# Sigmoid attention and a gated feed-forward: the first loads by SyncE in FP32, cast on ScalarE and VectorE, and the first pass in a new order

## The chip, the cores and the metric

The kernel runs on one core of one Trainium2 chip. The metric is the device time of one execution in microseconds. The time before is the median of three runs, 376.28 us (376.24 to 376.35). All positions below are microseconds from the start of the profiled span.

## What is computed

q, k and v have the shape (8, 12, 448, 64): 8 batches, 12 heads, 448 positions, 64 per head. All inputs and the output are FP32.

```python
scores = np.matmul(q, k.transpose(0, 1, 3, 2)) / np.sqrt(64) - np.log(448)
attn = 1 / (1 + np.exp(-scores))                 # a sigmoid, no softmax
x = np.matmul(attn, v)                           # heads put side by side: (3584, 768)
h = x @ w_in                                     # (3584, 2048)
out = (h / (1 + np.exp(-beta * h))) @ w_out      # (3584, 768)
```

## The kernel before, in words

**Tiles.** Heads are handled in 24 groups of four (three groups per batch). A group's q and k stand in one tile `raw` of 128 partitions, 32 for each head; each partition holds 14 blocks of 64 numbers. `load_one` (L122) loads q (in whole or one half of 7 blocks) or k of a group with a DMA that GpSimd issues and that turns FP32 into FP16 on the way. `transpose` (L201) makes `qT` and `kT` from it with VectorE's stream transposes (L207 for q; L216 and L220 for k, the first for 384 positions and the second for the last 64).

**A score visit.** `half_visit` (L294) does the scores of one group for one half of the queries (224 of 448). With `second` = 0 it does the first 256 keys, with `second` = 1 the other 192. It takes two pairs of PSUM banks, issues 16 matmuls of 32 rows (L236), and `weigh` (L247, ScalarE, L249) or `weigh_two` (L258, L264) writes the sigmoids to one or two of 14 slots of `attns`. At first three pairs of banks serve the scores (`share_psum(3)`), and from `("two",)` on two pairs.

**Values and the dense layers.** `attend` (L316) multiplies sigmoids with v (L334), and VectorE copies the result to `xT` (L343). `dense1` (L349) is the first dense layer in units of one matmul (L356); each sixth unit closes a block, whose sigmoid (ScalarE, L368) and product (VectorE, L371) go to the tile `gt`. `dense2` (L381, matmul L386) is the second layer. Later batches use products with fewer matmuls (L510, L628), which the change doesn't touch. All units of dense work stand in a list `fill`, in order; `fill_units(n)` issues the next n. The first batch has 48 units of 224 columns (blocks 0 to 7, first half of the queries), and then pairs of blocks at 448 columns, alternating with the other halves of earlier blocks.

**Order of the work.** Each engine runs its instructions in the order of the program, and this order is written out by hand. The first pass is the list `BEGIN` (L791): `("q", g, half)` and `("k", g)` are transposes, `("scores", g, half, second)` a score visit, `("values", g, half)` an `attend`, `("v", 0)` a copy inside v on VectorE (`double_v_last`, L168), `("beta",)` four small transposes, `("dense", n)` the next n units, and `("idle", n)` n matmuls on zeros (L751). Eleven more zero matmuls stand ahead of the list. Groups 0, 1 and 2 are one batch. After `BEGIN` a planner spreads the rest of `fill` over the visits of the later groups: it divides the work left by the number of visits left in a phase, with corrections by hand (`MORE`, `LATE`, L849 to L856).

**Loads.** GpSimd's queue carries, in this order: first half of q and all of k of group 0, two memsets, the list `LOADS` (L767), and at `("loads",)` those of `loads()` (L775). SyncE's queue carries one early load, `beta_in` (L766), and later all stores of the output. The tiles `raw` exist three times, so that group 3 takes the place of group 0.

Of the kernel before, what the change touches and what calls it, by code (L numbers as in the profile page):

```python
# [8 lines left out]
FP32 = mybir.dt.float32  # L9
FP16 = mybir.dt.float16  # L10
# [3 lines left out]
def kernel(  # L14
# [10 lines left out]
    nc = tc.nc  # L25
# [3 lines left out]
    B, H, S, D = q.shape  # L29
    NTOK, DM = out.shape  # L30
    DFF = moe_w_in.shape[1]
    P = 128
    BLK = 32
    HQ = P // BLK
    NB = S // BLK
# [19 lines left out]
    rawp = ctx.enter_context(tc.tile_pool(name="rawp", bufs=3))  # L55
# [29 lines left out]
    def bank(cols: int = S, hold=None, at=None):  # L85
        if at is None:
            at = min((i for i in used if i not in held.values()), key=used.get)
        assert at not in held.values()
        touch(at)
        if hold is not None:  # L90
            held[hold] = at
        width[at] = cols
        return ps[:, at, 0:cols]
# [25 lines left out]
    raws = {}  # L119
    vs = {}  # L120

    def load_one(g: int, r: int, c0: int = 0, c1: int = NB):  # L122
        b, t = divmod(g, QPB)
        if g not in raws:
            raws[g] = rawp.tile([P, 2, NB, D], FP16, tag="raw", name="raw")
        nc.gpsimd.dma_start(  # L126
            out=raws[g][:, r, c0:c1].rearrange("p c d -> p (c d)"),
            in_=(q, k)[r][b, HQ * t : HQ * (t + 1)].rearrange("h (p c) d -> (h p) (c d)", c=NB)[
                :, c0 * D : c1 * D
            ],  # L130
        )

    def load_qk(g: int):
        load_one(g, 0)
        load_one(g, 1)
# [7 lines left out]
    def load_v_full(b: int, lo: int = 0, hi: int = H):  # L143

        if b not in vs:
            vs[b] = vp.tile([P, H, JF + 1, D], FP16, tag="v16", name="v16")
        rows = v[b, lo:hi].rearrange("h (p c) d -> p h (c d)", c=NB)
        for i in range(HQ):
            nc.gpsimd.dma_start(
                out=vs[b][i * BLK : (i + 1) * BLK, lo:hi, 0:JF].rearrange("p h j d -> p h (j d)"),  # L150
                in_=rows[:, :, JF * i * D : JF * (i + 1) * D],
            )
            ready.update((b, "full", t, i) for t in range(lo // HQ, hi // HQ))

    def load_v_last(b: int):
        if b not in vs:
            vs[b] = vp.tile([P, H, JF + 1, D], FP16, tag="v16", name="v16")
        rows = v[b].rearrange("h (p c) d -> p h c d", c=NB)
        for c in range(NF, NB):
            lo = (c - NF) * BLK  # L160
            nc.gpsimd.dma_start(out=vs[b][lo : lo + BLK, :, JF], in_=rows[:, :, c])
        ready.add((b, "last"))

    def load_v(b: int):
        load_v_full(b)
        load_v_last(b)

    def double_v_last(b: int):  # L168
        assert (b, "last") in ready
        ready.add((b, "v"))  # L170
        nc.vector.tensor_copy(out=vs[b][KL:P, :, JF], in_=vs[b][0:KL, :, JF])
# [3 lines left out]
    def load_w_in(lo: int, hi: int):  # L175

        nc.gpsimd.dma_start(
            out=w_in16[:, :, lo * P : hi * P],
            in_=moe_w_in[:, lo * P : hi * P].rearrange("(c p) f -> p c f", p=P),
        )  # L180

    def load_w_out(c: int, half: int):
        n = NDC // WOUT
        cols = slice(half * HALF, (half + 1) * HALF)
        nc.gpsimd.dma_start(
            out=w_out16[:, c * n : (c + 1) * n, cols],
            in_=moe_w_out[c * n * P : (c + 1) * n * P, cols].rearrange("(c p) f -> p c f", p=P),
        )
# [5 lines left out]
    ready = set()  # L194


    def in_order(b: int, t):
        t = t.rearrange("p c e -> p (c e)").bitcast(FP32)
        return t.rearrange("p (q c) -> p c q", c=NB) if b == B - 1 else t

    def transpose(g: int, r: int, c0: int = 0, c1: int = NB):  # L201
        raw = raws[g][:, r]
        if r == 0:
            if g not in qT:
                qT[g] = qTp.tile([P, NB * BLK, PAIR], FP16, tag="qT", name="qT")
            ready.update((g, "q", c) for c in range(c0, c1, NB // 2))
            nc.vector.transpose(  # L207
                out=in_order(g // QPB, qT[g][:, c0 * BLK : c1 * BLK]),
                in_=raw[:, c0:c1].rearrange("p c d -> p (c d)").bitcast(FP32),
            )  # L210
            return
        ready.add((g, "k"))
        kT[g] = kTp.tile([P, S, PAIR], FP16, tag="kT", name="kT")
        to = kT[g].rearrange("p k e -> p (k e)").bitcast(FP32)
        frm = raw.rearrange("p c d -> p (c d)").bitcast(FP32).rearrange("p (c f) -> p c f", c=NB)
        nc.vector.transpose(  # L216
            out=to[:, 0 : JF * P].rearrange("p (j i q) -> p i j q", j=JF, i=HQ),
            in_=frm[:, 0:NF].rearrange("p (i j) f -> p i j f", j=JF),
        )
        nc.vector.transpose(  # L220
            out=to[:, JF * P :], in_=frm[:, NF:].rearrange("p c f -> p (c f)")
        )
# [123 lines left out]
    gt = const.tile([P, NDC, WIN], FP16, name="gt")  # L346
# [388 lines left out]
    NH = NB // 2  # L735
    share_psum(3)
    with tc.manual_schedule():
        load_one(0, 0, 0, NH)
        load_one(0, 1)
        nc.gpsimd.memset(nlogs, NEG_LOG_S)  # L740
        nc.gpsimd.memset(dummy, 0.0)
        nc.scalar.activation(out=dummy, in_=dummy, func=AF.Sigmoid, bias=0.0, scale=1.0)
# [4 lines left out]
        idle = bank(512)  # L747

        def idle_units(n: int):
            for _ in range(n):  # L750
                nc.tensor.matmul(idle, still[:, 0:P], still, start=True, stop=True)  # L751

        idle_units(11)
        def load(what, *a):
            if what == "q":
                load_one(a[0], 0, a[1] * NH, (a[1] + 1) * NH)
            elif what == "k":
                load_one(a[0], 1)
            elif what == "v":
                load_v_full(0, a[0] * HQ, a[1] * HQ)  # L760
            elif what == "last":
                load_v_last(0)
            elif what == "w_in":
                load_w_in(*a)

        nc.sync.dma_start(out=beta_in[0:NDC], in_=moe_beta.rearrange("(c p) -> c p", p=P))  # L766
        LOADS = [  # L767
            ("q", 1, 0), ("k", 1), ("q", 2, 0), ("k", 2), ("last",), ("v", 0, 3), ("q", 0, 1), ("q", 1, 1),
            ("w_in", 0, 2), ("w_in", 2, 4), ("q", 2, 1), ("w_in", 4, 6), ("w_in", 6, 8), ("w_in", 8, 10),
            ("w_in", 10, 12), ("w_in", 12, 14), ("w_in", 14, 16),  # L770
        ]
        for x in LOADS:
            load(*x)

        def loads():  # L775
            load_qk(3)
            load_w_out(0, 0)
            load_w_out(1, 0)
            load_v(1)
            load_qk(4)  # L780
            load_qk(5)
            load_w_out(0, 1)
            load_w_out(1, 1)

        def beta_columns():
            ready.add("beta")
# [2 lines left out]
                nc.vector.transpose(out=beta_sb[part], in_=beta_in[:, part])  # L789

        BEGIN = [  # L791
            ("q", 0, 0), ("k", 0), ("q", 1, 0), ("scores", 0, 0, 1), ("idle", 4), ("k", 1), ("idle", 4),
            ("scores", 0, 0, 0), ("k", 2), ("q", 2, 0), ("scores", 1, 0, 0), ("idle", 4), ("v", 0),
            ("scores", 1, 0, 1), ("scores", 2, 0, 0), ("values", 0, 0), ("q", 0, 1), ("q", 1, 1),
            ("scores", 2, 0, 1), ("beta",), ("values", 1, 0), ("scores", 0, 1, 0), ("values", 2, 0),
            ("scores", 0, 1, 1), ("loads",), ("q", 2, 1), ("dense", 12), ("scores", 1, 1, 1), ("two",),
            ("dense", 6), ("scores", 1, 1, 0), ("dense", 18), ("scores", 2, 1, 0), ("values", 0, 1),
            ("values", 1, 1), ("scores", 2, 1, 1), ("dense", 9), ("values", 2, 1), ("dense", 42), ("k", 3),
            ("q", 3, 0), ("q", 3, 1), ("dense", 21),
        ]  # L800
        for what, *a in BEGIN:
            if what == "q":
                g, half = a
                transpose(g, 0, half * NH, (half + 1) * NH)
            elif what == "k":
                transpose(a[0], 1)
            elif what == "scores":
                half_visit(a[0], a[1] * QH, a[2])
            elif what == "idle":
                idle_units(a[0])  # L810
            elif what == "v":
                double_v_last(a[0])
            elif what == "values":
                attend(a[0], a[1] * QH, QH, a[2:] or (0, 1))
            elif what == "dense":
                fill_units(a[0])
            elif what == "beta":
                beta_columns()
            elif what == "loads":
                loads()  # L820
            elif what == "two":
                share_psum(2)
# [153 lines left out]
```

## Time and profile before

| | before |
|---|---|
| median of three runs | 376.28 us |
| the profiled execution | 375.9 us |
| its span, first to last instruction | 374.1 us |
| TensorE busy | 366.0 us, 98% |
| ScalarE busy | 254.8 us, 68% |
| VectorE busy | 254.3 us, 68% |
| GpSimd busy | 91.4 us, 24% |
| first k of group 0: issue, landing | 1.95, 5.51 |
| first score matmul | 6.17 |
| first score sigmoid on ScalarE | 6.92 |
| start of the matmul run that goes on to the end | 30.86 |
| landing of k of group 1, of group 2 | 8.1, 10.1 |
| landing of w_in, first and last of eight pieces | 17.0, 32.4 |

A line of a timeline gives the start, the time, the engine, the line of the code, the operation, its output and inputs, and how many were merged; in brackets stands how long the engine had been idle before and what ended that. A line of the waits gives who waited for whom: the sum in us, the number of times, and the longest. In the page's rows of 40 slices, each digit is the busy share of one fortieth of the span, in tenths.

### The profile page before, as it was taken

The page shows a single profiled execution, that of the slowest core. Times are in us where ns is not written, and L with a number is a line of the kernel's source. Part 1 is how long each engine was busy: PE and PEld are TensorE (multiplying, and loading weights), DVE is VectorE, ACT ScalarE, POOL GpSimd, SP SyncE. Part 2 cuts the span into 40 slices and gives each one's busy share as a digit, 9 for nine tenths or more (in the row PEclk, how much of TensorE's full clock was granted, in tenths as well). Part 3 has the DMA queues.
Part 4 walks back from the last instruction along what each step waited for, and adds up shares of the span by engine and source line. Part 5 has one row for each costly group of instructions (what it writes and reads, how often), then busy time and mean ns, then how long its engine had stood idle before and what let it go on. Part 6 is the DMA issues. An engine that isn't in the chain of part 4 may idle for free.

```text
span 374.1 us, 7245 instructions
## 1 busy us (share of the span) xinstructions
PE 366.0 (98%) x2871; PEld 181.8 (49%) x2871; DVE 254.3 (68%) x479; ACT 254.8 (68%) x293; POOL 91.4 (24%) x138
## 2 busy tenths in 40 slices
PE   8799999999999999999999999999999999999996
PEld 3466544443444455544444455554444455555663
DVE  2444796776496967787666667778767657679662
ACT  3995866698967668886767748887677647882000
POOL 8833353141151013234123003235100002230000
PEclk9999999999999999999999999999999999999999
DMA  8999999993359030039839401028903111000333
GB/s 118 181 197 203 197 204 199 226 123 51 49 79 181 1 86 1 0 51 127 170 51 211 92 14 30 1 33 111 164 4 84 44 44 42 1 2 1 86 84 126
DMA packets 42402, 34.29 MB, mean 92 GB/s; under 512 B 21873, under 2 KB 38913, under 8 KB 42369
## 3 DMA queue, kind: packets, MB, share of 16 engines
q0 software_dynamic: 36976, 22.81, 44.7%
q1 hardware_dynamic: 5392, 11.02, 10.4%
q8 instruction: 22, 0.36, 0.4%
q14 instruction: 12, 0.09, 0.1%
HBM read 45.62 MB, written 11.01 MB: 151 GB/s over the span
## 4 chain that ended last, share of the span: by engine, by line
PE 91%; ACT 4%; DVE 2%; issue 1%; DMA 1%; POOL 0%; ACTq 0%; POOLq 0%
PE ps L628 27%; PE ps L510 26%; PE ps L236 11%; PE ps L334 9%; PE ps L356 9%; PE ps L386 4%; PE ps L424 4%; ACT attns L249 3%; DMA raw<-in_k_dram 1%; ACT sg L368 1%; PE ps L751 0%; ACT attns L264 0%; DVE sum L617 0%; DVE kT L216 0%; DVE qT L207 0%
## 5 line engine op out<-in xcount | busy, mean ns | idle before, releaser
L264 ACT ACTIVATE attns<-ps,nlogs 128x1792 f16<-128x1792 f32 x75 | 131.6, 1754 | 46.4 <-PE ps L236 46.1
L524 POOL TENSOR_TENSOR gt<-attns,sg 128x448 f16<-128x448 f32 x21 | 23.9, 1137 | 141.6 <-ACT sg L521 141.6
L628 PEld LDWEIGHTS <-sum 128*128 128x128 f16 x440 | 40.3, 98 | 36.7 <-issue 12.1
L236 PE MATMUL ps<-qT,kT 32*128 32x448 f16 (+3 forms) x864 | 51.7, 339 | 2.8 <-ACT attns L249 1.8
L521 ACT ACTIVATE sg<-ps,beta_sb 128x448 f32<-128x448 f32 x72 | 45.1, 631 | 8.6 <-PE ps L510 5.8
L510 PE MATMUL ps<-xT,w_in 128*128 128x448 f16 x216 | 49.2, 353 | 0.0
L510 PE MATMUL ps<-xT,w_S 128*128 128x448 f16 x216 | 49.2, 352 | 0.0
L628 PE MATMUL ps<-w_T,sum 128*128 128x384 f16 x264 | 48.5, 327 | 0.1
L524 DVE TENSOR_TENSOR gt<-ps,sg 128x448 f16<-128x448 f32 x72 | 44.3, 619 | 3.9 <-ACT sg L521 3.7
L343 DVE CAST xT<-ps 128x448 f16<-128x448 f32 (+1 forms) x54 | 28.8, 568 | 23.1 <-PE ps L334 22.9
L510 PEld LDWEIGHTS <-w_in 128*128 128x128 f16 x288 | 28.0, 98 | 26.6 <-issue 0.7
L646 DVE TENSOR_TENSOR osb<-ps,osb 128x384 f32<-128x384 f32 x55 | 30.5, 555 | 15.1 <-PE ps L628 13.2
L334 PE MATMUL ps<-attns,v 128*64 128x448 f16 (+3 forms) x432 | 40.5, 340 | 0.1
L356 PE MATMUL ps<-xT,w_in 128*128 128x448 f16 (+1 forms) x240 | 39.7, 316 | 0.6 <-DVE gt L371 0.6
L617 DVE TENSOR_TENSOR sum<-gt 128x1024 f16<-128x1024 f16 x55 | 36.6, 680 | 0.2
L126 POOL DMA_DIRECT2D raw<-in_q_dram x27 | 15.0, 557 | 82.9 <-DVE kT L220 74.5
L371 DVE TENSOR_TENSOR gt<-ps,sg 128x448 f16<-128x448 f32 (+1 forms) x40 | 19.8, 526 | 21.6 <-ACT sg L368 21.5
L628 PE MATMUL ps<-w_out,gt 128*128 128x384 f16 x176 | 33.5, 327 | 0.0
L628 PE MATMUL ps<-w_out,sum 128*128 128x384 f16 x176 | 32.3, 327 | 0.0
L570 DVE TENSOR_TENSOR ps<-ps,attns 128x448 f32<-128x448 f32 x24 | 15.2, 632 | 23.4 <-PE ps L510 23.4
L236 PEld LDWEIGHTS <-kT 32*128 32x128 f16 (+1 forms) x864 | 15.3, 96 | 31.6 <-issue 28.3
L510 PEld LDWEIGHTS <-w_S 128*128 128x128 f16 x216 | 21.1, 98 | 19.4
(50 smaller groups left out, 375.7 us busy)
## 6 DMA issues: line engine op xcount, KB each, us to landing
out_dram<-osb SPq DMA_DIRECT2D x98, 96.0 KB, 1.9
raw<-in_k_dram POOLq DMA_DIRECT2D x24, 224.0 KB, 5.3
raw<-in_q_dram POOLq DMA_DIRECT2D x21, 224.0 KB, 3.8
v<-in_v_dram POOLq DMA_DIRECT2D x32, 144.0 KB, 6.9
w_in<-in_moe_w_in_dram POOLq DMA_DIRECT2D x8, 384.0 KB, 10.9
w_out<-in_moe_w_out_dram POOLq DMA_DIRECT2D x4, 768.0 KB, 13.7
v<-in_v_dram POOLq DMA_DIRECT2D x16, 48.0 KB, 6.6
out_dram<-osb SPq DMA_DIRECT2D x2, 384.0 KB, 2.3
```

The source lines that it names most:

```text
L236: nc.tensor.matmul(sco[base : base + nk, hh, u0 : u0 + n], kT[g][lo : lo + BLK, jt * P : jt * P + nk, e], qT[g][lo : lo + BLK, c0 : c0 + n ...
L264: nc.scalar.activation(out=attns[:, slot : slot + 2].rearrange("p n h s -> p (n h) s"), in_=sco, func=AF.Sigmoid, bias=nlogs[:, 0:1], scal ...
L334: nc.tensor.matmul(av[hh * D : (hh + 1) * D, 0:n], vs[b][base : base + nk, 2 * (s % NPAIR) + hh, jt], at[base : base + nk, hh, 0:n], start ...
L343: nc.vector.tensor_copy(out=xTs[b][:, s % NPAIR, c0 : c0 + n], in_=av[:, 0:n])
L356: nc.tensor.matmul(m1, w_in16[:, hc, dc * P : (dc + 1) * P], xTs[b][:, hc, c0 : c0 + n], start=(hc == 0), stop=(hc == NHC - 1),)
L371: nc.vector.tensor_tensor(out=gt[:, dc, off : off + n], in0=m1, in1=sg[:, 0:n], op=ALU.mult)
L510: nc.tensor.matmul(out, w[:, c, i * P : (i + 1) * P], m[:, c], start=(start and c == 0), stop=(c == KH - 1), skip_group_check=not start,)
L521: nc.scalar.activation(out=sg, in_=h, func=AF.Sigmoid, bias=0.0, scale=beta_sb[:, dc : dc + 1])
L524: return lambda: engine.tensor_tensor(out=gt[:, dc, b % 2 * S : b % 2 * S + S], in0=h, in1=sg, op=ALU.mult)
L617: nc.vector.tensor_tensor(out=sums[t, i], in0=x, in1=y, op=op)
L628: nc.tensor.matmul(m2, (x if op is None else sums[t, i])[:, dc], w[:, dc], start=first, stop=(dc == ND - 1), skip_group_check=i >= 4,)
L646: nc.vector.tensor_tensor(out=out, in0=in0, in1=in1, op=op)
```

## The change

**Loads of group 0.** The first half of q (224 KB) and all of k (448 KB) are no longer loaded by GpSimd. SyncE loads them as FP32, ahead of `beta_in`, into a part of the tile `gt` that is not in use yet. A new step `cast` writes them to `raw` as FP16: ScalarE casts q (7 blocks, 448 columns) and blocks 8 to 13 of k (384 columns), VectorE casts blocks 0 to 7 of k (512 columns). The second half of q of group 0 is still loaded by GpSimd. The two memsets of GpSimd now stand ahead of all its DMAs.

**Zero matmuls.** Ten stand ahead of the first scores instead of eleven, and seven (1 + 3 + 3) between the visits instead of twelve (4 + 4 + 4).

**The first pass.** Group 0 does its two visits of the first query half directly one after the other, first 256 keys first. The visit (1, 0, 1) comes ahead of the copy inside v, (2, 0, 0) behind it as before. The transpose of the second half of group 2's q moves behind the visit (1, 1, 0). 120 dense units instead of 108 are issued in `BEGIN`, and 42 instead of 36 of them ahead of the last visit.

**Other loads.** In `LOADS` the v of groups 0 and 1 stands ahead of k of group 2, and that of group 2 behind the first piece of w_in. The later loads bring q and k of group 4 ahead of the second piece of w_out, and v of the next batch behind that piece.

```diff
-        load_one(0, 0, 0, NH)
-        load_one(0, 1)
-        idle_units(11)
+        LOADS = [
+            ("q", 1, 0), ("k", 1), ("q", 2, 0), ("v", 0, 2), ("k", 2), ("last",), ("q", 1, 1), ("q", 0, 1),
+            ("w_in", 0, 2), ("v", 2, 3), ("w_in", 2, 4), ("q", 2, 1), ("w_in", 4, 6), ("w_in", 6, 8),
+            ("w_in", 8, 10), ("w_in", 10, 12), ("w_in", 12, 14), ("w_in", 14, 16),
+        ]
+        LATER = [
+            ("qk", 3), ("w_out", 0, 0), ("qk", 4), ("w_out", 1, 0), ("values", 1), ("qk", 5), ("w_out", 0, 1),
+            ("w_out", 1, 1),
+        ]
+        staged = gt[:, 0:4].rearrange("p c w -> p (c w)").bitcast(FP32)
+        raws[0] = rawp.tile([P, 2, NB, D], FP16, tag="raw", name="raw")
+        parts = {0: (staged[:, NB * D :], NH), 1: (staged, NB)}
+        for r, (to, n) in parts.items():
+            nc.sync.dma_start(
+                out=to[:, 0 : n * D],
+                in_=(q, k)[r][0, 0:HQ].rearrange("h (p c) d -> (h p) (c d)", c=NB)[:, 0 : n * D],
+            )
+
+        def cast(r: int, c0: int, c1: int, act: bool):
+            out = raws[0][:, r, c0:c1].rearrange("p c d -> p (c d)")
+            frm = parts[r][0][:, c0 * D : c1 * D]
+            if act:
+                nc.scalar.copy(out=out, in_=frm)
+            else:
+                nc.vector.tensor_copy(out=out, in_=frm)
+            ready.update((r, "cast", c) for c in range(c0, c1))
...
         BEGIN = [
-            ("q", 0, 0), ("k", 0), ("q", 1, 0), ("scores", 0, 0, 1), ("idle", 4), ("k", 1), ("idle", 4),
-            ("scores", 0, 0, 0), ("k", 2), ("q", 2, 0), ("scores", 1, 0, 0), ("idle", 4), ("v", 0),
-            ("scores", 1, 0, 1), ("scores", 2, 0, 0), ("values", 0, 0), ("q", 0, 1), ("q", 1, 1),
-            ("scores", 2, 0, 1), ("beta",), ("values", 1, 0), ("scores", 0, 1, 0), ("values", 2, 0),
-            ("scores", 0, 1, 1), ("loads",), ("q", 2, 1), ("dense", 12), ("scores", 1, 1, 1), ("two",),
-            ("dense", 6), ("scores", 1, 1, 0), ("dense", 18), ("scores", 2, 1, 0), ("values", 0, 1),
-            ("values", 1, 1), ("scores", 2, 1, 1), ("dense", 9), ("values", 2, 1), ("dense", 42), ("k", 3),
-            ("q", 3, 0), ("q", 3, 1), ("dense", 21),
+            ("cast", 0, 0, 7, True), ("idle", 10), ("q", 0, 0), ("cast", 1, 0, 8, False),
+            ("cast", 1, 8, 14, True), ("k", 0), ("q", 1, 0), ("k", 1), ("scores", 0, 0, 0), ("scores", 0, 0, 1),
+            ("scores", 1, 0, 0), ("idle", 1), ("k", 2), ("q", 2, 0), ("idle", 3), ("scores", 1, 0, 1), ("v", 0),
+            ("idle", 3), ("scores", 2, 0, 0), ("values", 0, 0), ("q", 1, 1), ("q", 0, 1), ("scores", 2, 0, 1),
+            ("values", 1, 0), ("beta",), ("scores", 0, 1, 0), ("values", 2, 0), ("scores", 0, 1, 1),
+            ("dense", 12), ("scores", 1, 1, 1), ("two",), ("dense", 6), ("scores", 1, 1, 0), ("q", 2, 1),
+            ("dense", 24), ("loads",), ("scores", 2, 1, 0), ("values", 0, 1), ("values", 1, 1),
+            ("scores", 2, 1, 1), ("dense", 9), ("values", 2, 1), ("dense", 42), ("q", 3, 0), ("q", 3, 1),
+            ("k", 3), ("dense", 27),
         ]
```

## The prediction

> **What bounds the kernel now.** I read the page first, then the waits of TensorE in two halves of the span, then ScalarE in order of time over the first 33 us. The page:
>
> ```profile
> PE 366.0 (98%) x2871; PEld 181.8 (49%) x2871; DVE 254.3 (68%) x479; ACT 254.8 (68%) x293; POOL 91.4 (24%) x138
> PE   8799999999999999999999999999999999999996
> ```
>
> TensorE is busy almost everywhere; only the first three slices (28 us) are thinner, and part of that is zero matmuls. For 31 us to the end the view of TensorE's waits has no row at all. So from there on the end moves only with the moment at which the unbroken run of real matmuls starts and with the work that is left at that moment. Before 31 us the waits are these:
>
> ```profile
> PE ps L236 <- ACT attns L249: 1.8, 3, 1.0
> PE ps L751 <- DVE still L745: 1.2, 1, 1.2
> PE ps L356 <- DVE gt L371: 0.6, 1, 0.6
> ```
>
> Scores wait for ScalarE to empty their banks. ScalarE in order of time (start, us, line, count, idle before it):
>
> ```profile
> 6.92 1.53 ACT L249 ACTIVATE attns<-ps,nlogs 128x896 f16<-128x896 f32 x2 [4.05 <-PE ps L236]
> 9.24 11.98 ACT L249 ACTIVATE attns<-ps,nlogs 128x896 f16<-128x896 f32 x14 [0.79 <-PE ps L236]
> ...
> 25.18 1.15 ACT L368 ACTIVATE sg<-ps,beta_sb 128x224 f32<-128x224 f32 x3
> 26.16 1.80 ACT L264 ACTIVATE attns<-ps,nlogs 128x1792 f16<-128x1792 f32 x1
> 28.78 1.53 ACT L249 ACTIVATE attns<-ps,nlogs 128x896 f16<-128x896 f32 x2 [0.81 <-PE ps L236]
> ```
>
> From 6.92 on ScalarE is without work only for 0.79 and 0.81 us. Its last score sigmoid ends at 28.78 + 1.53 = 30.31, and the chain of waits goes on from it:
>
> ```profile
> 29.68 0.63 ACT attns L249
> 30.32 0.04 issue
> 30.36 0.51 PE ps L334 x6
> 30.86 9.53 PE ps L356 x63
> ```
>
> At 30.86 the unbroken run begins. The first pass is therefore bound by ScalarE, from its first score sigmoid, and that start comes from a load: in the same chain "DMA raw<-in_k_dram" runs from 1.95 to 5.51, then the k transpose (0.58), then scores at 6.17.
>
> **What the first score sigmoid waits for in the changed kernel.** Call its start s0 (6.92 before).
>
> SyncE's only early issue so far is
>
> ```profile
> 1.29 0.40 SPq L766 DMA_DIRECT2D beta_in<-in_moe_beta_dram  x1
> ```
>
> It waits for a memset that ends at 1.27. The new loads wait for nothing, so I put q at about 0.75 (ScalarE starts its table load at 0.74) and k one issue later, at 1.15. Nothing of SyncE's queue stands behind them but beta, read only near 16 us. The beta load landed 1.6 us after its issue. The page's other issues by SyncE, stores of 96 and 384 KB, took 1.9 and 2.3, so by that slope, (2.3-1.9)/288 per KB, 224 KB take about 2.1: q lands near 2.85. No row shows an FP32 load of this size, so k is bounded. Lower end: 448 KB by the same slope take 2.4, so 1.15 + 2.4, and some 0.35 behind q: 3.9. Upper end for the sum: the DMA rows by stretch show 176 to 192 GB/s between 3 and 7 us, counted as FP16 written, so about 360 KB/us read. First data at about 1.8 (the DMA rows of the first 6 us show beta's a microsecond after its issue); alone until GpSimd's q(1) starts to flow near 2.7, so 0.9 x 360 = 324 of the 672 KB; the other 348 at half the rate, if the two queues share evenly, 1.9 us: 4.6, and 0.4 until it is signalled (beta's 1.6 less the microsecond to its data and 0.2 or 0.3 of data): 5.0. I take 4.5, between them.
>
> The Trainium skill (DMA: Bandwidth & Descriptors, Queues, rings and completion order) says that every DMA engine serves its queues in turn, packet by packet, so a second queue brings no engines of its own. By that rule k would land at the 5.0 end and the sum would be 0.5 us poorer; the trace has no two loads on two queues to check it.
>
> Then the casts. Rows of ScalarE: 128x224 takes 0.45, 128x448 takes 0.63 (L368), so 384 columns of k cost 0.58; VectorE's CAST L343 takes 0.38 and 0.62, so 512 columns cost about 0.68. They run side by side: 0.65 to 0.7. The cast of q (0.63 on ScalarE) and its transpose (0.41) run between 2.85 and 3.9, under k's load; ScalarE was idle for 4.05 us here, and its dummy sigmoid is done near 2.1, since the memsets now stand ahead of GpSimd's DMAs. The trace has ScalarE copies (L556, L561) among sigmoids and a single table load, so the casts bring no second one. If the cover were gone, q's 1.04 would lie on the path. Behind the cast of k on VectorE stand only k's own transposes, then q(1) and k(1).
>
> Scores 0 0 0 need the first k transpose alone: 4.5 + 0.66 + 0.58 + 0.06 = 5.8. The ten zero matmuls, 0.43 each from 1.19, end at 5.5, so they don't decide; they would below k = 4.2. The scores to ScalarE took 0.56 (8.70 to 9.26). **s0 = 6.35**, floor 6.05 (zero matmuls).
>
> **ScalarE from there.** The eight score visits up to (0,1,1) are the same instructions in another order: 1.53 + 11.98 = 13.51. The idle 0.79 between them goes: it came from eight zero matmuls (1.83 us in the chain at 6.87) between the first two visits, and now two visits of group 0 follow each other directly. From 21.22 to 30.31 before: 9.09, with six dense sigmoids and the 0.81 gap, which stays, since the last visit needs the banks of the one before. Now there are seven dense sigmoids (12+6+24 units, 6 each): + 1.15/3 = 0.38. End: 6.35 + 13.51 + 9.09 + 0.38 = 29.33 against 30.31: **0.98 earlier**.
>
> **Dense work done by then.** Before the last values step 51 units are done instead of 45. Units 45 to 50 are three of 224 columns (1.90/18 = 0.106) and three of 448 (2.38/12 = 0.20): 0.92 us less behind the run's start. The last "dense 9" is 0.27 longer for the same reason; values began at 29.62 and their first ten matmuls, 0.56, were done 0.18 before the last sigmoid, so 0.09 of it shows. **Net 0.83.** The later 12+27+42 split is work of the unbroken run, and the planner's pace after it, fewer units per visit by 12, moves matmuls without adding any: zero.
>
> Sum: 0.98 + 0.83 = **1.8 us**. The profiled execution took 375.9 (span 374.1, and 1.8 around it); the runs' median is 376.28, 0.4 higher. Taken off the median: **374.5**.
>
> **What must arrive in time.** Landings from the issues' rows; the queue should be up to 0.9 us ahead, as data flows from 1.8 instead of 2.7. v(0,2), 384 KB, now stands ahead of k(2) (landed 10.1): + 2.0 - 0.9 = 11.2, transposed 12.0; its scores are wanted at s0 + 6.74 - 0.56 = 12.5. Cover 0.5. v(2,3) lands where w_in's first piece did, 17.0 - 0.9 = 16.1, wanted at 17.93 - 0.98 = 16.95. w_in's pieces keep their places from the second on. Of w_out's second piece (42.3), moved behind q and k of group 4: + 2.3 - 0.9 = 43.7, wanted when dense 2 passes its eighth row, near 45. The moved transposes of q and the beta columns fall on a VectorE that is busy 8.8 of 21.8 us.
>
> **Rivals.**
> 1. A late arrival: k(0) lands at 5.0 to 5.6, or k(2) loses its cover and stalls ScalarE by 0.4 to 0.8. For: the DMA engines are saturated from 3 us on, and FP32 writes twice the bytes. Against: the head start. Gain 0.7 to 1.4: 374.9 to 375.6.
> 2. Slower: the FP32 loads are bound by the bytes written, 190 KB/us, and not by those read. Alone from 1.8 to 2.7 they move 171 of the 672 KB, and the other 501 at half of 190 take 5.3: 8.0, landed 8.4. The way from k's landing to s0 is 0.66 + 0.58 + 0.06 + 0.56 = 1.86, so s0 = 10.25, which costs 3.9 against my forecast: 378.4. It turns at zero gain where s0 is 8.15, so where k lands later than 6.3; k's load before landed at 5.51.
> 3. Half clock. The first eleven zero matmuls took 4.75 / 11 = 0.43 each, the next eight 1.90 / 8 = 0.24, though the clock column prints full: TensorE starts slow and is released near 5.7. With 17 zero matmuls instead of 23 it could fall back in the first pass. Scores at 0.51 become 1.0, of which ScalarE's second tile (0.92 or 0.61) covers part: some 0.3 for each of eight visits and 0.2 for each of three values: 3.0. Time 377.5. Against: the longest idle gap so far, 1.0 us, did not do it, and the new one I count is about as long.
> 4. The edit changes nothing: the gain is given back to a stall before 45 us, w_out or v, so 375.9 to 376.6.
>
> On rival 3 the Trainium skill (TensorE: Matmul & The Clock Gate, What's actually happening) lets the clock fall only after an idle window of about 3.4 us. By that rule rival 3 is out; the trace agrees as far as it goes, with its 1.0 us.
>
> **How the numbers follow.** Forecast (gain 1.4 to 2.2): 0.52. More than that, up to 2.7, if k lands under 4.2 and a gap closes: 0.04. Rival 1: 0.22. Rival 4, with parts of the others that cancel: 0.10. Rival 2: 0.08. Rival 3: 0.04. About 0.2% (0.75 us) is what can be told from no change here. Forecast, more, and nearly all of rival 1 are faster by over that: 0.77; rival 4 is the same: 0.11; rivals 2 and 3 are slower: 0.12. The range goes from 373.7 to 376.0, through rival 1 and into rival 4; beyond it lie the slower cases and the rest of 4.
>
> **What would show it.** In the changed profile: ScalarE's first L249 at 6.05 to 6.9 and no idle of over 0.3 before it from there to the dense sigmoids; k's cast starting near 4.5; the unbroken run starting near 29.9 with 51 units done; no wait of TensorE after it. Wrong if k's cast starts after 6.3, if scores wait for the k(2) transpose, if sixteen scores take over 0.9 us, or if w_out appears among what TensorE waits for.

## The result: 0.9 us slower, and the profile after

The changed kernel takes 377.16 us (median of 14 runs, 376.68 to 377.70), the kernel before, run beside it, 376.25 (375.82 to 376.77). The ratio is 1.0022, with a 95% interval of 1.0014 to 1.0029: slower by 0.9 us, where 1.8 us less was forecast. The profiled execution took 377.22, its span 375.5.

First the page of the changed kernel: the busy times, and TensorE and its granted clock in 40 slices.

```profile
PE 366.2 (98%) x2865; PEld 181.1 (48%) x2865; DVE 255.0 (68%) x480; ACT 256.6 (68%) x295; POOL 92.6 (25%) x140
PE   6999999999999999999999999999999999999996
PEclk8799999999999999999999999999999999999999
```

TensorE looks better filled than before: the second slice has gone from 7 to 9. But the third row explains it: in the second slice the clock was granted at 0.7 only. Fuller here means slower matmuls. Cut at the edges of the clock's steps, which are 3.41 us apart, the first 18 us look like this (columns: stretch, length, busy time of PE, PEld, DVE, ACT and POOL, granted clock, DMA share, GB/s):

```profile
0.61:4.03 3.42, 2.83 (x7) 1.04 (x8) 0.40 (x2) 2.05 (x3) 2.87 (x7) 1.00 0.63 206
4.03:7.44 3.41, 1.54 (x22) 0.61 (x21) 1.99 (x6) 1.51 (x3) 2.56 (x5) 1.00 1.18 160
7.44:10.85 3.41, 2.54 (x31) 1.02 (x31) 0.66 (x2) 2.81 (x5) 3.19 (x6) 0.50 1.54 187
10.85:14.27 3.42, 3.42 (x23) 0.90 (x21) 1.50 (x4) 2.31 (x3) 3.20 (x6) 0.50 1.32 177
14.27:17.68 3.41, 3.41 (x66) 1.95 (x64) 1.30 (x4) 3.27 (x5) 2.29 (x4) 1.00 1.40 173
```

From 4.03 to 7.44 TensorE had work for 1.54 of 3.41 us, 45%, and then it ran at half clock for two stretches, up to 14.27. That is rival 3. Two of its waits lie in that stretch: 0.92 us for the k transpose, since with the release at 4.03 the zero matmuls ended at 4.91 and not at the 5.5 of the forecast, and 1.0 us for ScalarE. The same view of the kernel before, over the first two stretches behind its release, with the clock at 1.00 throughout:

```profile
5.68:9.09 3.41, 3.18 (x43) 1.38 (x43) 1.67 (x5) 1.53 (x2) 2.84 (x6) 1.00 1.16 171
9.09:12.50 3.41, 2.36 (x40) 0.93 (x33) 1.35 (x4) 3.25 (x4) 2.33 (x4) 1.00 1.67 183
```

Its thinner stretch holds 2.36 of 3.41, 69%. ScalarE in order of time in the changed kernel, in the columns of the prediction's view:

```profile
6.44 1.91 ACT L250 ACTIVATE attns<-ps,nlogs 128x896 f16<-128x896 f32 x2 [1.39 <-PE ps L237]
8.62 1.53 ACT L250 ACTIVATE attns<-ps,nlogs 128x896 f16<-128x896 f32 x2 [0.28 <-PE ps L237]
10.47 1.91 ACT L250 ACTIVATE attns<-ps,nlogs 128x896 f16<-128x896 f32 x2 [0.32 <-PE ps L237]
13.49 8.47 ACT L250 ACTIVATE attns<-ps,nlogs 128x896 f16<-128x896 f32 x10 [1.11 <-PE ps L237]
...
29.85 1.53 ACT L250 ACTIVATE attns<-ps,nlogs 128x896 f16<-128x896 f32 x2 [0.81 <-PE ps L237]
```

It starts 0.48 earlier (6.44, before 6.92) and then stands idle for 0.28 + 0.32 + 1.11 = 1.71 us. Its last score sigmoid ends at 29.85 + 1.53 = 31.38, before at 30.31. The chain of waits shows why it stands, and what comes after the pass (start, time, what):

```profile
9.68 0.93 PE ps L237 x13
10.61 1.82 PE ps L795 x4
12.42 1.01 PE ps L237 x13
13.43 1.18 PE ps L795 x3
14.61 0.51 PE ps L237 x16
...
31.38 0.35 ACT sg L369
31.73 0.02 issue
31.75 0.39 DVE gt L372
32.14 0.31 DVE xT L344
32.45 0.04 issue
32.49 9.77 PE ps L357 x68
```

Scores take 0.93 and 1.01 us and a zero matmul 1.82 / 4 = 0.45, until the scores of 14.61 are back at 0.51. The run to the end starts at 32.49, 1.63 later than before.

**Where the 0.9 us come from.** The run starts 1.63 later. From 68 us on each visit of a later group lies 0.96 later than before (the first compared 68.64 after 67.69, the last 301.26 after 300.30), and so does the last copy to the output (371.74 after 370.77). Between the two, 0.19 is added: at 53 us TensorE waits for the k transposes of group 4, which stand late on VectorE. So the dense units done before the run's start are worth 1.63 + 0.19 - 0.96 = 0.86.

**The other executions.** Every timed run has its mean granted clock over the span on record. One stretch of 3.41 us at half clock takes 3.41 / 2 / 375.5 = 0.45% off that mean; where no stretch fell, the profiles read 0.998 to 1.000, the rest being half clock behind the last matmuls. Of the 14 runs of the changed kernel 8 read 0.991, which is two stretches, and 6 read 0.995, which is one; their medians are 377.35 and 376.86. So the clock fell in every run, and the second stretch costs about 0.5 us. With only one, the time is still 0.6 above that of before. For the experiments the number of runs that fell is given; of 115 runs of the kernel before beside them, 7 fell.

### The profile page after: what moved, and what is told of

It is laid out like the page before. It is cut to its first block, busy times and chain, and to the rows that moved or that the text cites. A ratio compares the mean times of both kernels' runs of the same rounds, so it can differ in the third digit from the quotient of the medians.

```text
span 375.5 us, 7247 instructions
## 1 busy us (share of the span) xinstructions
PE 366.2 (98%) x2865; PEld 181.1 (48%) x2865; DVE 255.0 (68%) x480; ACT 256.6 (68%) x295; POOL 92.6 (25%) x140
## 4 chain that ended last, share of the span: by engine, by line
PE 91%; ACT 3%; DVE 3%; issue 1%; DMA 1%; SPq 0%; ACTq 0%; DVEq 0%
PE ps L629 27%; PE ps L511 25%; PE ps L237 12%; PE ps L335 9%; PE ps L357 9%; PE ps L425 4%; PE ps L387 4%; ACT attns L250 2%; DMA gt<-in_k_dram 1%; PE ps L795 1%; ACT sg L369 1%; ACT attns L265 0%; DVE kT L217 0%; DVE qT L208 0%; DVE sum L618 0%
## 5 line engine op out<-in xcount | busy, mean ns | idle before, releaser
L237 PE MATMUL ps<-qT,kT 32*128 32x448 f16 (+3 forms) x864 | 52.8, 345 | 3.4 <-ACT attns L250 1.8
```

Source lines behind the costliest of these rows:

```text
L237: nc.tensor.matmul(sco[base : base + nk, hh, u0 : u0 + n], kT[g][lo : lo + BLK, jt * P : jt * P + nk, e], qT[g][lo : lo + BLK, c0 : c0 + n ...
```

## The experiments

The edits below are to the changed kernel, where nothing else is said. Ratios are to the kernel before, run beside each, with the 95% interval, times are medians, and "later visits" are the shift of the visits of the later groups against before, in the two profiled executions. "Fell" counts the timed runs whose mean clock is 0.995 or lower. The theory is that the clock fell because TensorE had too little work in one stretch of 3.41 us. The rivals are that the loads came too late, and that the new order itself is the cost.

**Zero matmuls into the waits of the first visits.**

```diff
-("scores", 0, 0, 0), ("scores", 0, 0, 1), ("scores", 1, 0, 0),
+("scores", 0, 0, 0), ("idle", 4), ("scores", 0, 0, 1), ("idle", 6), ("scores", 1, 0, 0),
```

> The changed kernel with ten more zero matmuls where TensorE waits for ScalarE anyway: four between the two visits of group 0 and six behind them. Clock theory: in the changed kernel TensorE's clock fell to half from 7.4 to 14.3, since the stretch from 4.0 to 7.4 held only 1.57 us of work; with the waits filled it stays full, ScalarE loses its idle 0.28, 0.32 and 1.11, and the time is 375.2 to 375.8. Layout theory (the order of loads and the dense units cost the time, the clock is a bystander): within 0.3 of 377.2.

Measured: 376.63, 0.9999 (0.9985 to 1.0013), between the two expectations; fell in 0 of 12. By medians it is 0.4 above before (376.23 beside it), which the interval allows. In its profile, of one of the two fastest runs (376.00), the clock is released at 6.38 and doesn't fall again; later visits 0.30 earlier. ScalarE in order of time:

```profile
6.70 3.33 ACT L250 ACTIVATE attns<-ps,nlogs 128x896 f16<-128x896 f32 x4 [1.51 <-PE ps L237]
10.39 10.32 ACT L250 ACTIVATE attns<-ps,nlogs 128x896 f16<-128x896 f32 x12 [0.36 <-PE ps L237]
```

Of the 1.71 us of idle time 0.36 is left, and that comes from the six zeros, which are too many there. So ten zero matmuls more make the pass faster, and the clock holds in every run: the clock theory holds. But the forecast's gain doesn't come back, so the clock is not all of it.

**No zero matmuls between the visits.**

```diff
-("scores", 1, 0, 0), ("idle", 1), ("k", 2), ("q", 2, 0), ("idle", 3), ("scores", 1, 0, 1), ("v", 0), ("idle", 3),
+("scores", 1, 0, 0), ("k", 2), ("q", 2, 0), ("scores", 1, 0, 1), ("v", 0),
```

> The changed kernel without the 1 + 3 + 3 zero matmuls between the visits. Clock theory: the clock falls as before and stays low at least as long, since the stretches are emptier; the seven zeros at 0.43 leave TensorE's path (3.0 us), and ScalarE's 1.11 gap goes, so up to 1.0 is won, and lost again if the half clock reaches the dense units behind 20: 376.0 to 377.6, with the clock seen at half beyond 14.3. Layout theory: the zeros were all cost, the loads of k(2) and v decide, 376.0 to 376.4 and a clock that does not matter.

Measured: 377.97, 1.0037 (1.0023 to 1.0051), more than expected; fell in 10 of 11, in most for three stretches (0.984 to 0.986). The view by stretches:

```profile
5.69:9.10 3.41, 1.64 (x34) 0.86 (x35) 1.19 (x5) 2.68 (x3) 2.10 (x5) 1.00 1.36 178
9.10:12.52 3.42, 2.01 (x30) 0.93 (x29) 1.00 (x3) 2.82 (x5) 3.16 (x6) 0.50 1.38 168
12.52:15.93 3.41, 2.97 (x36) 1.76 (x40) 0.40 (x2) 3.09 (x4) 2.69 (x4) 0.50 1.35 167
15.93:19.35 3.42, 3.42 (x50) 1.78 (x44) 2.11 (x8) 1.63 (x3) 3.10 (x4) 0.50 1.26 165
```

With 48% of work the clock falls, and it stays down for three stretches instead of two: behind the first two, 59% and 87% full, it doesn't rise, behind the third it does. Later visits are 1.74 later, 0.8 more than in the changed kernel. Seven zeros that do nothing but keep TensorE busy were worth that.

**The loads alone.** FP32 by SyncE and the casts, with the order, the zeros and the loads lists of before:

```diff
 ("cast", 0, 0, 7, True), ("idle", 11), ("q", 0, 0), ("cast", 1, 0, 8, False), ("cast", 1, 8, 14, True), ("k", 0),
-("q", 1, 0), ("k", 1), ("scores", 0, 0, 0), ("scores", 0, 0, 1), ("scores", 1, 0, 0), ("idle", 1),
+("q", 1, 0), ("scores", 0, 0, 1), ("idle", 4), ("k", 1), ("idle", 4), ("scores", 0, 0, 0),
 ...
```

> The FP32 loads by SyncE and the casts alone, with the order, the zero matmuls (11 and 4 + 4 + 4) and GpSimd's loads of the kernel before. Clock theory: the eight zeros between the first visits keep the clock up; scores start 0.3 to 0.5 earlier and nothing else changes: 375.7 to 376.0. Rival (FP32 on a second queue hurts GpSimd's loads): k(1) and k(2) land later than 8.1 and 10.1, 376.3 or more.

Measured: 376.07, 0.9994 (0.9983 to 1.0005); just above the 376.0 expected; fell in 0 of 11. The scores start at 6.00 instead of 6.17, but at half rate (the release comes at 6.87), and the first sigmoid at 7.09, later than before; the idle 0.79 behind it is still there. So the loads cost nothing that shows, and alone they bring nothing that shows.

**The order alone.** The changed kernel with the first q and k of group 0 by GpSimd, as before:

```diff
-nc.sync.dma_start(out=to[:, 0 : n * D], ...)     # and the casts
+load_one(0, 0, 0, NH)
+load_one(0, 1)
```

> The new order, zero matmuls and loads with q and k of group 0 loaded by GpSimd as before, no casts. Clock theory: the zeros end near 5.5, TensorE waits, two visits follow each other, and the clock falls to half for one or two stretches of 3.4 us: slower than before by 0.5 to 2, 376.8 to 378.3. Rival (the order is good, the loads are bad): at or below 376.2.

Measured: 377.46, 1.0026 (1.0011 to 1.0041); fell in 11 of 12; later visits 1.72 later. The stretch from 5.49 holds 1.50 of 3.41 us of TensorE work (44%), and the clock is at half from 8.90 to 15.73. The loss sits in the order with its fewer zeros, not in the FP32 loads.

**Zeros, and the dense units placed anew.** Besides zeros as in the first run (4 and 4), three dense units move behind the last values step, so that none waits for its `xT`:

```diff
-("scores", 0, 0, 0), ("scores", 0, 0, 1), ("scores", 1, 0, 0),
+("scores", 0, 0, 0), ("idle", 4), ("scores", 0, 0, 1), ("idle", 4), ("scores", 1, 0, 0),
-("dense", 9), ("values", 2, 1), ("dense", 42),
+("dense", 6), ("values", 2, 1), ("dense", 45),
```

> The changed kernel with four zero matmuls between and four behind the visits of group 0 (four instead of six behind), and three of the dense units ahead of the last values step moved behind it (6 and 45 instead of 9 and 42). In the run before, six zeros made the next scores 0.36 late, and the first unit that reads the last values waited some 0.4 for VectorE's copy. Clock theory with these two small terms: clock full, ScalarE without the 0.36, the unbroken run without that wait, 0.7 less than with ten zeros: 375.3 to 376.0. Rival (something else of the new layout, later than 31, gives the gain back): 376.2 to 376.7.

Measured: 376.63, 1.0015 (1.0004 to 1.0026), within the rival's range; fell in 0 of 11. The wait for `xT` is gone, and yet the later visits are 0.36 later. ScalarE in order of time, then the waits of TensorE up to 31 us:

```profile
6.65 12.09 ACT L250 ACTIVATE attns<-ps,nlogs 128x896 f16<-128x896 f32 x14 [1.62 <-PE ps L237]
19.80 1.53 ACT L250 ACTIVATE attns<-ps,nlogs 128x896 f16<-128x896 f32 x2 [1.06 <-PE ps L237]
```

```profile
PE ps L795 <- DVE still L789: 1.2, 1, 1.2
PE ps L335 <- DMA v<-in_v_dram: 1.2, 1, 1.2
```

Fourteen tiles in one row are what the forecast counted on. Then ScalarE stands for 1.06, because TensorE waits 1.2 for v of group 2, which landed at 18.02. A second cause lies under the clock: the new list of loads has v(2, 3) behind a piece of w_in, and when the pass is fast, it can be wanted before it lands. In the changed kernel, at half clock, it landed at 16.60 and nobody waited; in the first run of this section it landed at 17.40, for a wait of 0.2. So the landing itself moves by up to 1.4 us. Here GpSimd had stood 1.41 at an issue (1.01 in the changed kernel), and from 12 to 13 us the DMA rows show 94 GB/s (160 there); that the one comes from the other is likely, not shown.

**Before, with fewer zeros.** The kernel before without the eight zeros between the first two visits:

```diff
-("scores", 0, 0, 1), ("idle", 4), ("k", 1), ("idle", 4), ("scores", 0, 0, 0),
+("scores", 0, 0, 1), ("k", 1), ("scores", 0, 0, 0),
```

> The kernel before without the eight zero matmuls between its first two score visits, nothing else changed. My prediction's step: ScalarE's idle 0.79 goes, the time falls to 375.5 to 376.0, k(2) and v being the next that are late. Clock theory: the stretch after the first release holds less than half its time in work, the clock falls to half for two stretches, and the time rises to 376.6 to 377.8.

Measured: 378.41, 1.0065 (1.0045 to 1.0085), slower than both expectations, with six runs between 376.86 and 379.75; fell in 5 of 6, by up to four stretches (0.982 at 379.75). The view by stretches:

```profile
6.75:10.16 3.41, 1.76 (x38) 0.78 (x42) 1.12 (x3) 2.67 (x4) 1.97 (x4) 1.00 1.28 166
10.16:13.57 3.41, 3.41 (x34) 1.14 (x33) 1.35 (x4) 2.58 (x3) 2.83 (x5) 0.50 1.61 188
```

Nothing of the change is in this kernel, and the clock falls behind a stretch with 52% of work. The eight zeros that the prediction booked as a pure loss of 0.79 us were what held the clock. The profiled execution is the fastest of the six, with one stretch, so its later visits, 0.97 later, are the least of the loss.

**Order and zeros, with the old first loads.** The kernel with zeros 4 and 4 and the dense units moved, but q and k of group 0 by GpSimd.

> The order alone (q and k of group 0 loaded by GpSimd as before, no casts) with the same zero matmuls and dense units as the first kernel of this set. Clock theory: the clock holds, and against the same order without those zeros 0.8 to 1.8 come back; what is left to the first kernel of this set is the later start of the scores, 0.2 to 0.6: 375.7 to 376.6. Rival (the loads by SyncE are what costs): below the first kernel of this set.

Measured: 377.44, 1.0034 (1.0022 to 1.0046): a miss, though the clock fell in only 1 of 8. Two of TensorE's waits up to 35 us, and then its first stretches:

```profile
PE ps L236 <- DVE kT L216: 1.2, 1, 1.2
PE ps L334 <- DVE beta_sb L793: 0.9, 1, 0.9
```

```profile
3.21:6.62 3.41, 2.43 (x6) 0.60 (x4) 0.87 (x2) 0.00 (x0) 3.41 (x7) 1.00 1.10 151
6.62:10.04 3.42, 3.24 (x32) 1.08 (x36) 1.28 (x5) 1.91 (x2) 1.42 (x3) 1.00 1.34 175
```

The ten zeros end at 5.6, k(0) is transposed 1.2 us later, and the stretch from 3.21 holds 71%: the clock was not released behind it but at 10.04, so the first visits ran at half rate although the clock had not fallen: it had not yet risen. That time isn't in the mean clock of a run, which is 0.999 here; a run with a long time and a mean of 1.00 can be such a case (one of the run without zeros took 379.30, one of before with fewer zeros 379.67). Here the FP32 loads do matter: they bring k earlier (in the same kernel with them the wait is 0.2 instead of 1.2). The second wait of 0.9 stands before the values of group 2: the profile puts it down to VectorE, while the weight load there waited 1.1 for v, which landed at 19.51. So this run loses at the start and at v, and its time is no price of the late k alone.

**v of group 2 earlier.** The kernel with zeros and dense units placed anew, and v(2, 3) ahead of the first piece of w_in:

```diff
-("w_in", 0, 2), ("v", 2, 3), ("w_in", 2, 4),
+("v", 2, 3), ("w_in", 0, 2), ("w_in", 2, 4),
```

> The run with eight more zeros and the moved dense units, and v of group 2 (v(2,3)) ahead of the first piece of w_in in GpSimd's queue. There TensorE waited 1.19 us for v(2,3), which landed at 18.0, and ScalarE stood idle 1.06. Theory (with the clock held, the loads of v bound the first pass): v(2,3) lands near 16, the idle goes, the unbroken run starts near 30.3: 375.2 to 375.8, faster than before. Rival (the gain is given back behind 31 or another load is late at once): 376.2 to 376.7.

Measured: 377.16, 1.0019 (1.0006 to 1.0032): a miss; fell in 0 of 12, so this loss is none of the clock's. ScalarE does all sixteen tiles in one row, and another wait has come up. ScalarE, then TensorE in order of time:

```profile
6.40 13.59 ACT L250 ACTIVATE attns<-ps,nlogs 128x896 f16<-128x896 f32 x16 [1.46 <-PE ps L237]
```

```profile
25.65 0.75 PE L357 MATMUL ps<-xT,w_in 128*128 128x224 f16 x6 [1.47 <-DMA w_in<-in_moe_w_in_dram]
```

The fourth piece of w_in lands at 25.60 (before: 24.21), and dense units want it 1.47 us earlier. From 12 to 15 us the DMA rows show 93 GB/s instead of some 180. From 10.96 to 11.45 GpSimd had waited, before an issue, for the landing of k(2); that the gap comes from there is likely, not shown.

**v of group 2 earlier, alone.** The changed kernel with that edit of the loads and no more zeros:

> The changed kernel with v(2,3) ahead of the first piece of w_in, and nothing else. Theory: with TensorE at half clock its values come at 18.5, later than v lands anyway, so nothing changes: 376.8 to 377.4, clock at half for two or three stretches. Rival (the load of v costs the time, not the clock): 376.0 to 376.5.

Measured: 377.04, 1.0023 (1.0009 to 1.0038); fell in 12 of 12. In the profile the clock falls behind a stretch with 1.92 of 3.41 us (56%) and is at half from 10.39 to 13.80. So the place of v doesn't repair the fall; and the new lists don't make it, as the kernel before with fewer zeros fell with the old ones.

**The loads, with the old zeros moved.** The loads-alone kernel, with four of its eight early zeros behind the second visit:

```diff
-("scores", 0, 0, 1), ("idle", 4), ("k", 1), ("idle", 4), ("scores", 0, 0, 0), ("k", 2),
+("scores", 0, 0, 1), ("idle", 2), ("k", 1), ("idle", 2), ("scores", 0, 0, 0), ("idle", 4), ("k", 2),
```

> The FP32 loads alone with the order of the kernel before, and four of the eight zero matmuls between the first two visits moved behind the second visit, where TensorE waits 1.0 for ScalarE; as many zeros as before. If only the place of the zeros makes ScalarE's idle 0.79 and their number keeps the clock: clock full, the idle gone, 0.5 to 0.8 less than with the loads alone: 375.2 to 375.7, faster than before. If the loads bind the pass (as v(2,3) and w_in's fourth piece did in the new order): the gain is lost at one of them, 375.9 to 376.5.

Measured: **375.43, 0.9979 (0.9965 to 0.9992)**, faster than the kernel before, and so than the changed one; fell in 1 of 11 (376.75). ScalarE:

```profile
7.13 13.58 ACT L250 ACTIVATE attns<-ps,nlogs 128x896 f16<-128x896 f32 x16 [2.12 <-PE ps L237]
```

Sixteen tiles without a gap, though the order is the old one: the 0.79 goes with the same number of zeros, if they stand where TensorE waits anyway. In the profile the clock is released at 7.10 and holds. Later visits 0.52 earlier.

**Before, with the zeros moved.** The same move without the FP32 loads:

> The kernel before with the same four zeros moved, no other change. If place and number of the zeros are what matters: clock full, ScalarE's idle 0.79 gone, 375.4 to 375.8. If the loads bind: 375.9 to 376.5, with a wait of TensorE for v or w_in. If four zeros in this place do not hold the clock: over 376.8.

Measured: 376.77, 1.0011 (1.0000 to 1.0022); fell in 7 of 12. The profiled execution is the fastest of the twelve: there the clock holds and the idle 0.79 is gone, but the visits come only 0.10 earlier, as TensorE now waits 0.4 for v (landed 14.18). The median is another matter. The seven runs in which the clock fell, for one stretch by their mean of 0.994 or 0.995, took 376.73 to 377.31, median 376.91; the five others have a median of 375.90. So without the FP32 loads these zeros hold the clock in some executions only, and one stretch at half clock costs 1.0 here. Why it falls so much more often than with the FP32 loads (7 of 12 against 1 of 11) is not shown, as no fallen execution was profiled.

**The old lists of loads.** The kernel with zeros and dense units placed anew, and both lists of loads as before:

```diff
-("q", 2, 0), ("v", 0, 2), ("k", 2), ("last",), ("q", 1, 1), ("q", 0, 1), ("w_in", 0, 2), ("v", 2, 3),
+("q", 2, 0), ("k", 2), ("last",), ("v", 0, 3), ("q", 0, 1), ("q", 1, 1), ("w_in", 0, 2),
```

> The run with eight more zeros and the moved dense units, but GpSimd's lists of loads from the kernel before: v whole ahead of w_in, k(2) ahead of v, the later loads in the old order. The new order of the visits and the FP32 loads stay. If the new list of loads is what stops the new order once the clock is held: no wait for v(2,3) or w_in, unbroken run from near 30.3, 375.2 to 375.8. If the loads bind whatever their order: a wait for v or w_in elsewhere, 376.0 to 377.

Measured: 375.77, 0.9991 (0.9982 to 1.0000); fell in 0 of 11. ScalarE in order of time, then the chain of waits:

```profile
6.46 13.60 ACT L250 ACTIVATE attns<-ps,nlogs 128x896 f16<-128x896 f32 x16 [1.50 <-PE ps L237]
```

```profile
28.86 0.64 ACT attns L250
29.49 0.04 issue
29.54 0.51 PE ps L335 x6
30.04 10.37 PE ps L357 x72
```

This is the first pass that the prediction described: s0 at 6.46 (6.35 forecast), the last score sigmoid at 29.49 (29.33), the run from 30.04 (29.9), though with 48 units done instead of 51. Later visits 0.89 earlier at first, 0.80 at the end. Against the run with zeros and dense units placed anew, only the lists of loads differ: they cost 0.24% there (1.0015 against 0.9991). This profile is better than that of the loads with the zeros moved (0.80 against 0.52), but the timed ratios stand the other way, and their intervals overlap; the one profile is of the fastest run of eleven (375.48), the other of the second slowest (375.78). Which of the two versions is the better stays open.

## Why the prediction was wrong

**Right: the way to the first sigmoid.** SyncE issued at 0.74 and 1.18, as forecast; k landed at 4.52 (4.5 forecast), q at 3.44 instead of 2.85, under k's load; the casts took 0.56, 0.51 and 0.54; s0 came at 6.44 (6.35).

```profile
0.74 0.39 SPq L770 DMA_DIRECT2D gt<-in_q_dram  x1
1.18 0.42 SPq L770 DMA_DIRECT2D gt<-in_k_dram  x1
```

k(2) landed at 11.25 (11.2) and stalled nobody. The rule of the Trainium skill (DMA: Bandwidth & Descriptors, Queues, rings and completion order) put k at the 5.0 end; it landed 0.5 us before that; whether the rule or the rates that went with it were off, no run tells. Rivals 1 and 2 are out: from 3 to 4 us the DMA rows show 372 GB/s, before 176, so the FP32 loads are not bound at the 190 KB/us of rival 2. The forecast's reading of 176 to 192 GB/s between 3 and 7 us left out a row of 129 from 5 to 6; nothing here hangs on it.

**The step that failed: "Against: the longest idle gap so far, 1.0 us, did not do it, and the new one I count is about as long."** Rival 3 was set aside by the length of single gaps. TensorE's longest wait between 4.03 and 7.44 was indeed about 1.0 us, and the clock fell. What counts in these runs is the share of work in a stretch of 3.41 us: 45% here, where the kernel before had 69%. The row was there to be read: the view by stretches gives it for before, and for the planned order the work could have been added up from durations that the prediction had. That rival 3's time came out so near (377.5 forecast, 377.2 measured) is in part luck: its 3.0 us counted half clock for the whole first pass, while the half clock cost some 2.0 (the last score sigmoid ended at 31.38 and not at 29.33) and the steps below another 0.7. The Trainium skill (TensorE: Matmul & The Clock Gate, What's actually happening), by whose rule "rival 3 is out", lets the clock fall only after an idle window. No window here was idle; the trace disagrees, and the measurement decides: a window 44 to 56% full was enough.

**"The idle 0.79 between them goes."** The eight zeros in front of it were priced as a loss without a use. Taken away, they made the kernel before slower by 0.65% instead of saving 0.79 us. With four of them moved to where TensorE waits for ScalarE, the gap does go. From s0 to the last score sigmoid 22.98 was forecast, 24.94 measured, 23.03 in the run with the old lists, where the clock holds. Of the 1.91 between the last two, 1.71 is ScalarE's idle time.

**"Net 0.83" for more units done.** The units were done early (0.86 in the account above), but the fifth of the block behind the last values reads their `xT`, which VectorE writes behind the last dense product. The values' matmuls end at 31.89, the run starts at 32.49, and one unit of 0.20 lies between: 0.40 lost. The prediction asked what ScalarE's end releases, and not what the added units read. With three units fewer in front (48), the wait is gone.

**"The queue should be up to 0.9 us ahead."** v(2, 3) landed at 16.60 instead of the forecast 16.1, the second half of q(2) at 21.53 (before 20.27), the last piece of w_in at 32.91 (32.28). By 36 us GpSimd's queue had moved 5.87 MB; before, 6.19 with the 0.34 of group 0, which is 5.85 without. So the head start of group 0 was group 0's alone. At half clock nothing waited for these. With the clock held, the new list costs the 1.2 us wait for v, and with v ahead the 1.5 us wait for w_in. That is rival 4's mechanism, and it takes much of the gain even without rival 3: zeros against the fall of the clock bring back 0.5 us by medians and 0.9 by the ratios (1.0022 to 0.9999 in the first run), which ends at no gain.

**"Moves matmuls without adding any: zero."** The 0.19 at 53 us is a wait that this step didn't see. It is there with the old lists of loads too (at 51 us), so it belongs to the new order of the dense units and transposes; it was not taken apart further. And even in the run with the old lists, where the pass goes as forecast, the gain is 0.8 to 0.9 and not 1.8: 0.82 from the start of the run, 0.29 from three more units, less the 0.19, 0.9 by this account. The forecast had all of 51 units done at that start.

**What stays open.** The stretches begin at another point in each execution: the release was seen between 4.03 and 7.10 us, and at 10.04 once. A kernel whose stretches are near the threshold falls in one execution and not in another (7 of 12 in before with the zeros moved, 7 of 115 in before itself). In which stretch an unprofiled run fell, and when its clock first rose, is not seen. Runs that didn't fall still differ by up to 2.3 us (376.02 to 378.28 with the dense units placed anew); what makes that was not taken apart. Why the same load lands up to 1.4 us apart from kernel to kernel is open too.

## What to carry to other kernels

Before you remove dummy matmuls or let a tensor engine wait for another engine, add up its work over every stretch of the clock's length, dummies included, and don't go by the longest gap: here each stretch at half clock cost 0.5 to 1.0 us, and the zeros that prevented it cost nothing where the engine waited anyway. Keep their number and move them, and count them before the release as well as after. Read the mean clock of every run, and not the profiled one's alone: one profile can show a clock that holds in a kernel whose median run falls. When a pass gets faster, check each load behind it against its new due time, since a list of loads that fits a slow pass hides its own waits.

## What the runs showed of the hardware

**The clock fell by the share of work.** It fell behind stretches with 44, 45, 48, 52 and 56% of TensorE work, and held behind one with 57% (1.95 of 3.42 us from 23.10, with v of group 2 earlier) and all with 65% or more. It rose behind 83% (0.61 to 4.03 in the changed kernel) and behind all with 92% or more. It did not rise behind 59, 71 and 74% (the last is 7.44 to 10.85 in the changed kernel), nor, in one case each, behind 82 and 87%. So the share alone doesn't settle the rise, and as busy time is modelled, these are no exact thresholds. The clock column reads 1.00 in the first microseconds too, though zero matmuls take 0.43 there and 0.24 later: before the first release the durations tell the rate, the column doesn't.

**FP32 loads by SyncE.** In the changed kernel 224 KB took 2.7 us from issue to landing and 448 KB 3.3, one behind the other, and beta's 8 KB behind both 4.6 instead of 1.6 (3.4 to 5.5 in the other runs with these loads). That costs nothing here because beta is read late.

**GpSimd can stand at an issue.** In the changed kernel an issue of v stood 1.01 us, by the profile until an earlier load, of k, had landed; with v of group 2 ahead one stood 0.49 us. Whether the 93 GB/s between 12 and 15 us of that run come from it is not shown.
